# Retention scores and token transposes as 64 by 64 quarters of TensorE, with the decay put on q

## The chip, the core and the metric

One core of one Trainium2 chip runs the whole program once. The metric is the device time of one execution in microseconds (us); the median of three runs counts. On the core, TensorE (PE) multiplies matrices and writes to the eight banks of PSUM, VectorE (DVE) and ScalarE (ACT) read PSUM, GpSimd (POOL) works on SBUF alone, and SyncE (SP) issues most transfers. Each engine takes its instructions in program order and waits on semaphores for the others.

## What is computed

Three stages follow each other: retention (linear attention with a decay per head), a top-1 mixture of eight experts, and a dense layer with squared ReLU. The change lies in the first.

```python
# retention: B, H, S, D = 8, 8, 576, 64
scores = scale * np.matmul(q, k.transpose(0, 1, 3, 2))
gamma = 1.0 - 2.0 ** (-5.0 - np.arange(H))
Dmat = np.where(rel >= 0, gamma[:, None, None] ** rel, 0.0)      # rel = query - key position
x = matmul(scores * Dmat, v)                                     # -> 4608 tokens of 512 features
# experts: N, D, E, F = 4608, 512, 8, 1024
logits = x @ w_gate + modality_bias[modality_id]
out[token] = gate_w * (relu(x @ w1[e]) @ w2[e])                  # e = argmax(logits)
# dense: h = relu(x @ w_in); return h * h @ w_out
```

## The kernel before

The retention stage is `phase0`. The 4608 tokens are 36 tiles (`t`) of 128 tokens; 9 tiles hold 2 sequences of 576, so tile 4 of each 9 (`tt == 4`) holds the end of one sequence and the start of the next. The 512 features are four chunks `c` of 128, each with two heads `i` of 64. Four tiles make a group `g` for loading (`alloc`, `load`: k and q transposed, v and k natural, 1 MB each) and for routing (`route_a` to `route_c`). All products of this stage are of 32-bit floats, and each appears as two weight loads and two matmuls in the trace (so 8 products are "x16").

Per tile, TensorE does five things. `qk(t)` (L507) forms the scores of each head: 64 rows by 128 columns of the array, so two products side by side, 128 columns moving. DVE masks them into `at` (L510), two instructions of 512 elements. `om(t)` first adds the state product (L528), 64 by 64 quarters, four side by side, then scores times values (L534), 128 by 64. DVE multiplies the result by the decay `odec` into `xt` (L542, L545). `kv(t)` (L561) updates the state, which ACT copies to `sbs` (L564). `xm(t)` (L577) multiplies `xt` by `iwg`, an identity beside the gate's weights: a full 128 by 128 product with 136 columns moving for each chunk, which turns the tokens to rows and yields the logits. ACT copies the logits to `lp` (L579) and the tokens to `xs` (L580). POOL scales the values into `vh` (L500) and, in `prep`, builds `bias` and `trib` (L617 to L627).

The loop of L645 runs t from 0 to 36. In iteration t the order on every engine is: loads of a group ahead (where t % 4 is 1), `qk(t+1)`, `om(t)`, `kv(t)`, the steps that `stage` holds for this iteration (`route_c`, L252, four full-array products of 288 columns), `xm(t-1)`. The routing of a group, `route_a` (15 steps, mostly small DVE instructions, with an exponential and four `xs` scalings L199 to L207 on ACT) and `route_b` (10 steps; the first is a pair of products L215 and L216 into a bank of the ring of banks 6 and 7), is handed out in small parts: `adv(n)` runs n steps, three inside `qk` after each mask and three after `om`. After `xm(4g+3)` in iteration 4g+4 `route_a(g)` is queued, two iterations later `route_b(g)`, and in iteration 4g+8 `route_c(g)` runs.

At the end (t = 32 to 36) the routing of group 7 runs in one go, its table gives the first expert (`early`), and POOL gathers that expert's first tokens (`gather("E")`, four indirect transfers L453 after the copy of L450). `phase12` begins with their transposes (L768) and the expert's first products (L815). The later stages, 185 us to the end, are not touched by the change other than through the order of the rows of w1, which is permuted outside the kernel.

Of the kernel before, what the change touches and what calls it, by code (L numbers as in the profile page):

```python
# [32 lines left out]
LC = P + NE  # L33
# [11 lines left out]
def consts():  # L45
# [9 lines left out]
    od[1::2] = od[1::2, ::-1].copy()  # L55
# [36 lines left out]
def kernel(ctx, tc, qT, kT, kN, vN, modT, w_gate, mbias, w1, w2, w_in, w_out,  # L92
# [16 lines left out]
    banks = [bp.tile([P, TS], F32, name=f"bank{i}") for i in range(8)]  # L109
# [14 lines left out]
    psX = Banks(g=[6, 7])  # L124
    ring = [psX]
# [21 lines left out]
    def bc(ap, shape):  # L147
        return ap.to_broadcast(shape)
# [62 lines left out]
    def route_b(g, eng):  # L211
        t0 = G * g
        oh, pm = OH[g]
        ps = ring[0].tile([P, G, NE], F32, tag="g", name="psr")
# [42 lines left out]
    def tab_turn():  # L257
        tf = s1.tile([P, KEYS], F32, tag="tf", name="tf")
        ti = s1.tile([KEYS // 3, 3, P], I32, tag="ti", name="ti")
        dve.tensor_scalar(out=tf, in0=tps, scalar1=IDOFF, scalar2=None, op0=ALU.add)  # L260
        yield
        ps = ring[0].tile([P, 3, P], F32, tag="g", name="pst3")[:KEYS // 3]
        for j in range(3):
            pe.transpose(ps[:, j, :], tf[:, KEYS // 3 * j:KEYS // 3 * (j + 1)], ident)
        yield
        dve.tensor_copy(ti, ps)
        sp.dma_start(td.rearrange("(j k) b -> k j b", j=3), ti)
        yield

    def count(t, name):  # L270
        ps = ring[0].tile([P, NE], F32, tag="g", name=name)
        pe.matmul(ps, trib[:, 1, :], acc[:, t, :], start=True, stop=True, skip_group_check=True)
        return ps
# [183 lines left out]
    def phase0():  # L457
        with ExitStack() as c0:
# [13 lines left out]
            sps = psY.tile([P, KD, D], F32, tag="y3", name="sps")  # L472
# [21 lines left out]
            def qk(t, adv):  # L494
                b_, a, vn, kn = U[t // 4]
                x = t % 4
                cs = slice(x * P, x * P + P)
                at = wk.tile([P, H, P], F32, tag="at", name="at")
                vh = wk.tile([P, H, D], F32, tag="vh", name="vh")
                pool.tensor_tensor(out=vh, in0=vn[:, x, :].rearrange("p (h d) -> p h d", h=H),  # L500
                                   in1=bc(vdec[:, t % 9, :].unsqueeze(2), [P, H, D]), op=ALU.mult)
                mk = mask[:, 1 if t % 9 == 4 else 0, :]
                ps = [psY.tile([P, KD, P], F32, tag=f"y{i}", name=f"psa{i}") for i in range(2)]
                for c in range(KD):
                    for i in range(2):
                        r0 = 64 * i
                        pe.matmul(ps[i][:, c, :], b_[r0:r0 + 64, c, cs], a[r0:r0 + 64, c, cs],  # L507
                                  start=True, stop=True, skip_group_check=True)
                for i in range(2):
                    dve.tensor_tensor(out=at[:, KD * i:KD * i + KD, :], in0=ps[i],  # L510
                                      in1=bc(mk.unsqueeze(1), [P, KD, P]), op=ALU.mult)
                    adv(3)
                AT[t], VH[t] = at, vh
# [3 lines left out]
            def om(t):  # L517
                b_, a, vn, kn = U[t // 4]
                x = t % 4
                at, vh = AT[t], VH[t]  # L520
                pso = [banks[i][:, :2 * P].rearrange("p (c t) -> p c t", c=2) for i in (2, 5)]
                tt = t % 9
                ns = 0 if tt == 0 else (64 if tt == 4 else P)
                sb = sbs[scur[0]]
                for a2 in range(0, KD if ns else 0, 2):
                    for c, i in ((a2, 0), (a2 + 1, 1), (a2 + 1, 0), (a2, 1)):
                        o = 64 * (i ^ (c & 1))
                        pe.matmul(pso[c & 1][o:o + 64, c // 2, :ns], sb[64 * i:64 * i + 64, c, :],  # L528
                                  a[64 * i:64 * i + 64, c, x * P:x * P + ns], start=(a2 == 0), stop=False,
                                  skip_group_check=True)  # L530
                for c in range(KD):
                    for o in (0, 64):
                        i = (o // 64) ^ (c & 1)
                        pe.matmul(pso[c & 1][o:o + 64, c // 2, :], vh[:, 2 * c + i, :], at[:, KD * i + c, :],  # L534
                                  start=(c < 2 and not ns), stop=(c >= 2), skip_group_check=True)
                xt = wk.tile([P, KD, P], F32, tag="xt", name="xt")
                xv = xt.rearrange("p (c b) t -> p b c t", b=2)
                p0 = (t * P) % S
                n = min(P, S - p0)
                for b in range(2):  # L540
                    od = odec[:, b::2, :]
                    dve.tensor_tensor(out=xv[:, b, :, :n], in0=pso[b][:, :, :n], in1=od[:, :, p0:p0 + n],  # L542
                                      op=ALU.mult)
                    if n < P:
                        dve.tensor_tensor(out=xv[:, b, :, n:], in0=pso[b][:, :, n:], in1=od[:, :, 0:P - n],  # L545
                                          op=ALU.mult)
                XT[t] = xt

            def kv(t):
# [3 lines left out]
                b_, a, vn, kn = U[t // 4]  # L553
                x = t % 4
                vh = VH[t]
                r0 = 64 if tt == 4 else 0
                new = tt in (0, 4)
                for c in range(KD):
                    for i in range(2):
                        h = 2 * c + i  # L560
                        pe.matmul(sps[64 * i:64 * i + 64, c, :], kn[r0:, x, h * D:h * D + D], vh[r0:, h, :],  # L561
# [4 lines left out]
            def xm(t):  # L566
                g, j = t // G, t % G
                if j == 0:
                    XS[g] = wp.tile([P, G, DM], F32, tag="w", name="xs")
                    LP[g] = sm.tile([P, G, KD, NE], F32, tag="lp", name="lp")  # L570
                xt = XT.pop(t)
                xs = XS[g][:, j, :].rearrange("p (c d) -> p c d", c=KD)
                for a in range(2):
                    ps = psX.tile([P, 2, LC], F32, tag="g", name="psx")
                    for i in range(2):
                        c = 2 * a + i
                        pe.matmul(ps[:, i, :], xt[:, c, :], iwg[:, c, :], start=True, stop=True,  # L577
                                  skip_group_check=True)
                    act.activation(LP[g][:, j, 2 * a:2 * a + 2, :], ps[:, :, P:], AF.Copy)  # L579
                    act.activation(xs[:, 2 * a:2 * a + 2, :], ps[:, :, :P], AF.Copy)  # L580
# [3 lines left out]
            load(0, 0, 1, both, (0, 1))  # L584
            load(0, 1, 1, both, (0, 1))
            sp.dma_start(mask, mats_d[:, 0:2 * P].rearrange("p (a b) -> p a b", a=2))
            act.dma_start(vdec, vdec_d)
            load(0, 0, 1, both, (2, 3))
            sp.dma_start(odec[:, :, 0:P], odec_d[:, :, 0:P])
            act.dma_start(ident, mats_d[:, 2 * P:3 * P])  # L590
            for i in range(2):
                wgs = w_gate.rearrange("(c b p) e -> p c b e", b=2, p=64)
                for b in range(2):
                    act.dma_start(iwg[64 * i:64 * i + 64, b::2, P:], wgs[:, b::2, i ^ b])
            load(0, 1, 1, both, (2, 3))
            load(0, 2, 2, parts=(0, 1))
            sp.dma_start(odec[:, :, P:256], odec_d[:, :, P:256])
# [7 lines left out]
            noadv = lambda n: None  # L605
            qk(0, noadv)
            for c in range(KD):
                if c % 2 == 0:
                    pool.tensor_copy(iwg[:, c, :P], ident)
                else:  # L610
                    pool.tensor_copy(iwg[:, c, :64], ident[:, 64:])
                    pool.tensor_copy(iwg[:, c, 64:P], ident[:, :64])
# [32 lines left out]
            for t in range(NTILE + 1):  # L645
# [9 lines left out]
                if t == 2:  # L655
                    work.append(prep())
                if t + 1 < NTILE:
                    qk(t + 1, adv)
                if t < NTILE:
                    om(t)  # L660
# [18 lines left out]
                    kv(t)  # L679
                for it, fn in list(stage.items()):  # L680
                    if it == t:
                        fn()
                if t >= 1 and t - 1 != xl_:
                    xm(t - 1)
                    g, j = (t - 1) // G, (t - 1) % G
                    if j == G - 1 and g < NG - 2:
                        work.append(wrap(route_a(g)))
                        stage[t + 2] = lambda g=g: work.append(wrap(route_b(g, dve)))
                        stage[t + 4] = lambda g=g: (adv(99), route_c(g))

    def phase12():
        ring[0] = psG
# [681 lines left out]
def lay_out(i):  # L1374
    c = np.ascontiguousarray
    vdec, odec, mats, rows, _ = consts()
    tr = lambda a: c(a.transpose(1, 3, 0, 2)).reshape(DM, NT)
    nat = lambda a: c(a.transpose(0, 2, 1, 3)).reshape(NT, DM)
    return {
        "qT": tr(i['q']), "kT": tr(i['k']), "kN": nat(i['k']), "vN": nat(i['v']),  # L1380
        "modT": c(i['moe_modality_id'].astype(np.int64).reshape(NTILE, P).T),
        "w_gate": c(i['moe_w_gate']), "mbias": c(i['moe_modality_bias']),
        "w1": c(i['moe_w1']), "w2": c(i['moe_w2']),
# [18 lines left out]
```

## Time and profile before

| | us |
|---|---|
| median of 3 runs (1371.52 to 1373.61) | 1372.58 |
| the profiled execution | 1375.41 |
| its span, first to last instruction | 1373.6 |
| PE busy in the span | 1334.8 (97%) |
| DVE, ACT, POOL busy | 1022.4, 627.4, 131.0 |
| granted clock, mean | 0.995 |

A timeline row gives the start, the time that it is busy, the engine, the line, the operation, the tiles and how many instructions are merged. The busy time of a matmul row holds the modelled end of the last one; the time that a kind of work takes TensorE is the distance from its start to the start of the next row. Rows of one line are merged over an engine's neighbouring instructions. A row of the grouped view gives the count, the total, the mean of one in ns, and the idle time of the engine just before with what ended it.

### The profile page before, as it was taken

The page shows a single profiled execution, that of the slowest core. Times are in us where ns is not written, and L with a number is a line of the kernel's source. Part 1 is how long each engine was busy: PE and PEld are TensorE (multiplying, and loading weights), DVE is VectorE, ACT ScalarE, POOL GpSimd, SP SyncE. Part 2 cuts the span into 40 slices and gives each one's busy share as a digit, 9 for nine tenths or more (in the row PEclk, how much of TensorE's full clock was granted, in tenths as well). Part 3 has the DMA queues.
Part 4 walks back from the last instruction along what each step waited for, and adds up shares of the span by engine and source line. Part 5 has one row for each costly group of instructions (what it writes and reads, how often), then busy time and mean ns, then how long its engine had stood idle before and what let it go on. Part 6 is the DMA issues. An engine that isn't in the chain of part 4 may idle for free.

```text
span 1373.6 us, 26947 instructions
## 1 busy us (share of the span) xinstructions
PE 1334.8 (97%) x10643; PEld 1228.3 (89%) x10643; DVE 1022.4 (74%) x2077; ACT 627.4 (46%) x1283; POOL 131.0 (10%) x170
## 2 busy tenths in 40 slices
PE   6999999999999999999999999999999999999997
PEld 5888877888888888879999999999999999999997
DVE  2787857878787787554888888867887777776765
ACT  1444444454445445444655555543344344443333
POOL 3222114101110110000000000000000011111121
PEclk9999999999999999999999999999999999999999
DMA  9988256778786886669545554577799756564451
GB/s 332 386 303 295 91 195 231 272 278 283 246 288 236 302 277 216 240 232 342 226 187 207 211 212 185 207 269 270 288 337 339 279 229 209 200 213 170 169 183 48
DMA packets 139380, 332.55 MB, mean 242 GB/s; under 512 B 15568, under 2 KB 50160, under 8 KB 139248
## 3 DMA queue, kind: packets, MB, share of 16 engines
q1 hardware_dynamic: 131120, 310.21, 63.1%
q0 software_dynamic: 5920, 19.40, 4.0%
q8 instruction: 84, 1.38, 0.4%
q10 hardware_dynamic: 2208, 1.17, 0.3%
q14 instruction: 48, 0.39, 0.1%
HBM read 222.59 MB, written 108.17 MB: 241 GB/s over the span
## 4 chain that ended last, share of the span: by engine, by line
PE 47%; DMA 3%; DVE 2%; ACT 0%; issue 0%; POOL 0%; SPq 0%; POOLq 0%
PE bank L1176 16%; PE bank L1174 16%; PE bank L1175 16%; DMA w<-wc 3%; DVE z L1152 1%; DVE h L1277 0%; DVE z L1160 0%; ACT h L1276 0%; POOL out L1284 0%; SPq L1047 0%; DVE oe L1152 0%; ACT z L1149 0%; DVE x L1152 0%; DVE yr L1152 0%; POOLq L1398 0%
## 5 line engine op out<-in xcount | busy, mean ns | idle before, releaser
L1174 PE MATMUL bank<-x,w 128*128 128x256 f32 x1008 | 285.9, 284 | 1.2 <-ACT z L1149 1.1
L1175 PE MATMUL bank<-w,h 128*128 128x256 f32 x1008 | 282.8, 281 | 3.7 <-DMA w<-wc 3.7
L1175 PE MATMUL bank<-x,w 128*128 128x256 f32 x1008 | 285.8, 284 | 0.5 <-DVE x L1152 0.5
L1174 PE MATMUL bank<-w,h 128*128 128x256 f32 x1008 | 282.7, 280 | 2.9 <-DVE oe L1152 1.6
L1176 PE MATMUL bank<-x,w 128*128 128x256 f32 x1008 | 285.0, 283 | 0.0
L1176 PE MATMUL bank<-w,h 128*128 128x256 f32 x1008 | 282.2, 280 | 0.7 <-DVE h L1277 0.7
L1149 ACT ACTIVATE z<-bank 128x256 f32<-128x256 f32 x288 | 108.7, 380 | 255.5 <-PE bank L1176 253.5
L1174 PEld LDWEIGHTS bank<-x,w 128*128 128x128 f32 x1008 | 192.6, 191 | 2.7 <-ACT z L1149 2.7
L1276 ACT ACTIVATE h<-z 128x512 fp32r<-128x512 f32 (+2 forms) x270 | 158.2, 598 | 80.0 <-DVE z L1152 63.7
L1175 PEld LDWEIGHTS bank<-x,w 128*128 128x128 f32 x1008 | 192.9, 191 | 1.1 <-DVE x L1152 0.7
L1174 PEld LDWEIGHTS bank<-w,h 128*128 128x128 f32 x1008 | 190.0, 189 | 4.0 <-DVE oe L1152 2.2
L1175 PEld LDWEIGHTS bank<-w,h 128*128 128x128 f32 x1008 | 189.6, 188 | 4.4 <-DMA w<-wc 4.3
L1176 PEld LDWEIGHTS bank<-x,w 128*128 128x128 f32 x1008 | 193.1, 192 | 0.0
L1176 PEld LDWEIGHTS bank<-w,h 128*128 128x128 f32 x1008 | 189.7, 188 | 0.9 <-DVE h L1277 0.9
L1277 DVE TENSOR_TENSOR h<-z,h 128x512 fp32r<-128x512 f32 (+2 forms) x270 | 168.7, 648 | 7.8 <-ACT h L1276 7.8
L1152 DVE TENSOR_TENSOR z<-z,bank 128x256 f32<-128x256 f32 x216 | 89.2, 416 | 68.8 <-PE bank L1176 50.0
L815 PE MATMUL bank<-hh,wy 128*128 128x512 f32 (+1 forms) x320 | 125.3, 392 | 0.0
L815 PE MATMUL bank<-xh,wx 128*128 128x512 f32 (+1 forms) x320 | 122.9, 384 | 1.7 <-DVEq L934 1.7
L816 PE MATMUL bank<-xl,wx 128*128 128x512 f32 (+1 forms) x320 | 122.7, 383 | 1.1 <-DVE xl L771 1.1
L817 PE MATMUL bank<-xh,wx 128*128 128x512 f32 (+1 forms) x320 | 123.5, 386 | 0.0
L817 PE MATMUL bank<-hh,wy 128*128 128x512 f32 (+1 forms) x320 | 123.3, 385 | 0.0
L816 PE MATMUL bank<-hl,wy 128*128 128x512 f32 (+1 forms) x320 | 122.6, 383 | 0.0
(172 smaller groups left out, 2135.9 us busy)
## 6 DMA issues: line engine op xcount, KB each, us to landing
x<-xc SPq DMA_DIRECT2D x112, 512.0 KB
wr<-w SPq DMA_DIRECT2D x80, 512.0 KB
xc<-x SPq DMA_DIRECT2D x63, 512.0 KB
w<-wc SPq DMA_DIRECT2D x32, 896.0 KB
wc<-cwh SPq DMA_DIRECT2D x16, 896.0 KB
wc<-cwl SPq DMA_DIRECT2D x16, 896.0 KB
pd<-oe SPq DMA_DIRECT2D x24, 512.0 KB
xd<-xs SPq DMA_DIRECT2D x9, 1024.0 KB
```

The source lines that it names most:

```text
L815: pe.matmul(ps, lh, rh, start=first, stop=False)
L816: pe.matmul(ps, lh, rl, start=False, stop=False)
L817: pe.matmul(ps, ll, rh, start=False, stop=last)
L1149: plan.add(a_(c), lambda e: e.activation(o, i, f), r, w)
L1152: plan.add(engs or d_(c), lambda e: e.tensor_tensor(out=o, in0=a, in1=b, op=op), r, w)
L1174: e.matmul(ps[n], lh, rh, start=first and n == 0, stop=False, skip_group_check=True)
L1175: e.matmul(ps[n], lh, rl, start=False, stop=False, skip_group_check=True)
L1176: e.matmul(ps[n], ll, rh, start=False, stop=True, skip_group_check=True)
L1276: plan.add(a_(c), lambda e: e.activation(h[:, 0, a:b], z[:, a + 1:b + 1], AF.Copy), rs, ks[0])
L1277: plan.add(d_(c), lambda e: e.tensor_tensor(out=h[:, 1, a:b], in0=z[:, a + 1:b + 1], in1=h[:, 0, a:b].bitcast(F32), op=ALU.subtract), rs + ...
```

## The change

`qk` computes the scores in quarters: for each chunk and head, and each half `h` of the 128 keys, a 64 by 64 product with 128 columns moving; 16 products in place of 8. `xm` does the same for the tokens: for each chunk, half of the tokens and head, a 64 by 64 product with 72 columns moving (64 of an identity, 8 of the gate); 16 in place of 4. `iwg` comes ready from the host, and the gate's partial logits double (`lp` has 2 * KD parts). The order in an iteration becomes `ahead(t+2)`, `qk(t+1)`, `sq_(t)` (the state product), `adv(6)`, `stage`, `xm(t-1)`, `om(t)` (scores times values), `kv(t)`, `adv(3)`. The decay is no longer multiplied into `xt`: `ahead` multiplies it into q, in place, on DVE for the first four tiles and on POOL after that, and also makes `vh`, two iterations before the tile's own. `xt` becomes one ACT copy of 512 elements out of two banks, and the copies of `xm` become one of 64 and one of 512 elements. The banks are laid out anew: scores 0 and 1, result 2 and 3, state 5, tokens and logits 6 and 7, the small routing products in the rest of bank 6. The first transfers are reordered, with the first piece of `odec` ahead of the second tile.

```diff
-LC = P + NE
+LC = D + NE
...
-    psX = Banks(g=[6, 7])
-    ring = [psX]
+    def route_bank(shape, name):
+        if side[0]:
+            n = int(np.prod(shape[1:]))
+            ps = banks[6][:, KD * LC:KD * LC + n]
+            return ps.rearrange("p (a b) -> p a b", b=NE) if len(shape) == 3 else ps
+        return psG.tile(shape, F32, tag="g", name=name)
...
+            psa = bank[:, 0:2, :].rearrange("p i (c t) -> p i c t", c=KD)
+            pso = bank[:, 2:4, :2 * P].rearrange("p b (c t) -> p b c t", c=2)
+            sps = banks[5][:, :KD * D].rearrange("p (c d) -> p c d", c=KD)
+            psx = bank[:, 6:8, :KD * LC].rearrange("p b (c e) -> p b c e", c=KD)
...
+            def ahead(t):
+                if t < NTILE:
+                    a = U[t // 4][1][:, :, t % 4 * P:t % 4 * P + P]
+                    e = dve if t < 4 else pool
+                    p0 = (t * P) % S
+                    n = min(P, S - p0)
+                    e.tensor_tensor(out=a[:, :, :n], in0=a[:, :, :n], in1=odec[:, :, p0:p0 + n], op=ALU.mult)
+                    if n < P:
+                        e.tensor_tensor(out=a[:, :, n:], in0=a[:, :, n:], in1=odec[:, :, 0:P - n], op=ALU.mult)
+                    vh = VH[t] = wk.tile([P, H, D], F32, tag="vh", name="vh")
+                    pool.tensor_tensor(out=vh, in0=U[t // 4][2][:, t % 4, :].rearrange("p (h d) -> p h d", h=H),
+                                       in1=bc(vdec[:, t % 9, :].unsqueeze(2), [P, H, D]), op=ALU.mult)
...
+                for c in range(KD):
+                    for h in range(2):
+                        ks = slice(t % 4 * P + 64 * h, t % 4 * P + 64 * h + 64)
+                        for i in range(2):
+                            pe.matmul(psa[64 * h:64 * h + 64, i, c, :], b_[D * i:D * i + D, c, ks],
+                                      a[D * i:D * i + D, c, cs], start=True, stop=True, skip_group_check=True)
                 mk = mask[:, 1 if t % 9 == 4 else 0, :]
...
-                    dve.tensor_tensor(out=xv[:, b, :, :n], in0=pso[b][:, :, :n], in1=od[:, :, p0:p0 + n],
-                                      op=ALU.mult)
...
+                xt = XT[t] = wk.tile([P, 2, 2, P], F32, tag="xt", name="xt")
+                act.activation(xt, pso, AF.Copy)
...
+                for c in range(KD):
+                    for h in range(2):
+                        for r in range(2):
+                            pe.matmul(psx[64 * h:64 * h + 64, r, c, :],
+                                      xt[D * r:D * r + D, c & 1, c // 2, 64 * h:64 * h + 64],
+                                      iwg[D * r:D * r + D, c, :], start=True, stop=True, skip_group_check=True)
+                act.activation(LP[g][:, j].rearrange("p (r c) e -> p r c e", r=2), psx[:, :, :, D:], AF.Copy)
+                act.activation(XS[g][:, j, :].rearrange("p (r c d) -> p r c d", r=2, c=KD), psx[:, :, :, :D], AF.Copy)
...
+                ahead(t + 2)
                 if t + 1 < NTILE:
-                    qk(t + 1, adv)
+                    qk(t + 1)
                 if t < NTILE:
-                    om(t)
+                    ns = sq_(t)
+                    adv(6)
+                for it, fn in list(stage.items()):
+                    if it == t:
+                        fn()
+                if t >= 1 and t - 1 != xl_:
+                    xm(t - 1)
...
+                if t < NTILE:
+                    om(t, ns)
+                    kv(t)
```

## Rows read from the trace of the kernel before

**Rows 1.** Busy time by stretch: bounds, length, then each engine's, clock, DMA.

```profile
35.00:153.00 118.00, 117.28 (x1886) 103.67 (x1884) 89.88 (x302) 49.20 (x164) 28.22 (x27) 1.00 0.81 293
```

**Rows 2.** Timeline of TensorE, iterations 20 and 21: start, busy time, instructions.

```profile
107.83 0.79 PE L252 MATMUL bank<-okb 128*128 128x288 f32 x4
108.46 1.09 PE L577 MATMUL bank<-iwg,xt 128*128 128x136 f32 x8
109.48 1.16 PE L507 MATMUL bank<-q,k 64*128 64x128 f32 x16
110.57 0.67 PE L528 MATMUL bank<-q,sbs 64*64 64x128 f32 x16
111.17 1.09 PE L534 MATMUL bank<-at,vh 128*64 128x128 f32 x16
112.09 0.64 PE L561 MATMUL bank<-vh,kn 128*64 128x64 f32 x16
112.66 1.19 PE L577 MATMUL bank<-iwg,xt 128*128 128x136 f32 x8
113.78 0.49 PE L507 MATMUL bank<-q,k 64*128 64x128 f32 x3
```

**Rows 3.** Timeline of TensorE, iteration 31 (state product with 64 columns).

```profile
152.91 1.16 PE L507 MATMUL bank<-q,k 64*128 64x128 f32 x16
...
154.15 0.46 PE L528 MATMUL bank<-q,sbs 64*64 64x64 f32 x16
154.54 1.09 PE L534 MATMUL bank<-at,vh 128*64 128x128 f32 x16
...
158.58 1.16 PE L507 MATMUL bank<-q,k 64*128 64x128 f32 x16
```

**Rows 4.** Groups of instructions by line and shape, 35 to 153 us.

```profile
L510 DVE TENSOR_TENSOR at<-bank,mask 128x512 f32<-128x512 f32 x54 | 36.8, 684 | 26.6 <-PE bank L507 26.6
...
L500 POOL TENSOR_TENSOR vh<-v,vdec 128x512 f32<-128x512 f32 x27 | 28.3, 1047 | 90.0 <-PE bank L561 59.5 <-issue 21.5 <-PE bank L534 5.6
...
L580 ACT ACTIVATE xs<-bank 128x256 f32<-128x256 f32 x53 | 19.8, 380 | 0.0
L542 DVE TENSOR_TENSOR xt<-bank,odec 128x256 f32<-128x256 f32 x48 | 17.9, 413 | 0.0
...
L202 ACT ACTIVATE xs<-xs,gg 128x512 f32<-128x512 f32 x7 | 4.9, 707 | 0.0
```

**Rows 5.** Waits, 35 to 153 us: who for whom, total us, times, longest.

```profile
PE bank L215 <- ACT xs L580: 0.7, 1, 0.7
```

**Rows 6.** Timeline, a POOL instruction beside a small one of DVE.

```profile
94.81 1.04 POOL L500 TENSOR_TENSOR vh<-v,vdec 128x512 f32<-128x512 f32 x1 [3.32 <-issue]
95.01 0.89 DVE L180 TENSOR_TENSOR sh<-lg,mx 128x32 f32<-128x32 f32 x1
```

**Rows 7.** All instructions of L180: shortest, median and longest, ns.

```profile
L180 DVE TENSOR_TENSOR sh<-lg,mx x9: 180/183/890, 42.2 to 193.5; 128x32 f32<-128x32 f32 x9
```

**Rows 8.** Timeline, the start of the stage.

```profile
23.36 0.40 POOL L617 CAST trib<-trio 128x256 bf16<-128x256 f32 x1 [4.09 <-DMA trio<-mats]
...
25.11 0.79 POOL L627 TENSOR_TENSOR bias<-bias,bias 128x288 f32<-128x288 f32 x1
...
28.87 1.47 PE L507 MATMUL bank<-q,k 64*128 64x128 f32 x16 [3.41 <-DMA q<-qT]
...
31.58 3.23 POOL L500 TENSOR_TENSOR vh<-v,vdec 128x512 f32<-128x512 f32 x3 [5.68 <-DMA v<-vN]
...
34.73 1.16 PE L507 MATMUL bank<-q,k 64*128 64x128 f32 x16
```

**Rows 9.** Timeline, the end of the stage and the first expert.

```profile
171.43 0.19 POOL L450 COPY ix<-tab 128x4 int32 x1 [13.98 <-DVE eslot L298]
...
177.39 1.05 POOL L500 TENSOR_TENSOR vh<-v,vdec 128x512 f32<-128x512 f32 x1
178.49 0.85 PEld L534 LDWEIGHTS bank<-at,vh 128*64 128x64 f32 x16 [3.04 <-POOL vh L500]
...
183.11 1.95 PE L768 MATMUL bank<-ident,xg 128*128 128x128 f32 x16
184.81 0.48 PE L815 MATMUL bank<-xh,wx 128*128 128x512 f32 x1
```

More of the change, by code (lines that the diff above doesn't have):

```diff
@@ L107 @@
     s1 = cm.enter_context(tc.tile_pool(name="s1", bufs=1))
-    banks = [bp.tile([P, TS], F32, name=f"bank{i}") for i in range(8)]
+    bank = bp.tile([P, 8, TS], F32, name="bank")
+    banks = [bank[:, i, :] for i in range(8)]
     class Banks:
@@ L261, in tab_turn @@
         yield
-        ps = ring[0].tile([P, 3, P], F32, tag="g", name="pst3")[:KEYS // 3]
+        ps = psG.tile([P, 3, P], F32, tag="g", name="pst3")[:KEYS // 3]
         for j in range(3):
@@ L509, in qk, with sq_ @@
                 for i in range(2):
[L510 to L513, printed above, removed]
+                    dve.tensor_tensor(out=at[:, i], in0=psa[:, i], in1=bc(mk.unsqueeze(1), [P, KD, P]), op=ALU.mult)
             scur = [0]
[L517 to L521, printed above, removed]
+            def sq_(t):
+                a = U[t // 4][1]
@@ L569, in xm @@
                     XS[g] = wp.tile([P, G, DM], F32, tag="w", name="xs")
-                    LP[g] = sm.tile([P, G, KD, NE], F32, tag="lp", name="lp")
+                    LP[g] = sm.tile([P, G, 2 * KD, NE], F32, tag="lp", name="lp")
                 xt = XT.pop(t)
[L572 to L580, printed above, removed]
+                for c in range(KD):
[6 more added lines that the diff above has]
+                act.activation(XS[g][:, j, :].rearrange("p (r c d) -> p r c d", r=2, c=KD), psx[:, :, :, :D], AF.Copy)
             alloc(0)
@@ L584, in phase0 @@
             load(0, 0, 1, both, (0, 1))
+            sp.dma_start(odec[:, :, 0:P], odec_d[:, :, 0:P])
+            act.dma_start(vdec, vdec_d)
+            act.dma_start(mask, mats_d[:, 0:2 * P].rearrange("p (a b) -> p a b", a=2))
+            load(0, 0, 1, both, (2, 3))
             load(0, 1, 1, both, (0, 1))
[L586 to L594, printed above, removed]
+            sp.dma_start(odec[:, :, P:256], odec_d[:, :, P:256])
+            act.dma_start(iwg, iwg_d.rearrange("p (c e) -> p c e", c=KD))
             load(0, 1, 1, both, (2, 3))
             load(0, 2, 2, parts=(0, 1))
-            sp.dma_start(odec[:, :, P:256], odec_d[:, :, P:256])
+            act.dma_start(ident, mats_d[:, 2 * P:3 * P])
             load(0, 2, 2, parts=(2, 3))
@@ L604, in phase0 @@
             dve.memset(acc[:, 0, :], 0.0)
[L605 to L612, printed above, removed]
+            ahead(0)
+            qk(0)
+            ahead(1)
             alloc(1)
@@ L656, in phase0 @@
                     work.append(prep())
+                ahead(t + 2)
                 if t + 1 < NTILE:
-                    qk(t + 1, adv)
+                    qk(t + 1)
                 if t < NTILE:
-                    om(t)
+                    ns = sq_(t)
[5 more added lines that the diff above has]
+                    xm(t - 1)
+                    g, j = (t - 1) // G, (t - 1) % G
+                    if j == G - 1 and g < NG - 2:
+                        work.append(wrap(route_a(g)))
+                        stage[t + 2] = lambda g=g: work.append(wrap(route_b(g, dve)))
+                        stage[t + 4] = lambda g=g: (adv(99), route_c(g))
+                if t < NTILE:
+                    om(t, ns)
+                    kv(t)
                     if t == xl_ + 2:
@@ L678, in phase0 @@
                             pass
[L679 to L689, printed above, removed]
     def phase12():
-        ring[0] = psG
+        side[0] = False
         with ExitStack() as c1:
```

64 lines of the change are left out of this document (24 added, 40 removed).

## The prediction, before the changed kernel was run

> **What bounds the kernel now.** I read the busy time by stretch first. From 35 to 153 us, where the retention loop runs undisturbed, TensorE is busy 117.28 of 118.00 us at full clock, DVE 89.88, ACT 49.20, POOL 28.22 [rows 1]. So time falls where TensorE's work falls, until DVE's 76% becomes the bound. Then I read TensorE's timeline: the distance from one row to the next is what a kind of work takes. Iteration 21 is a plain one: scores 1.09 us, state product 0.60, scores times values 0.92, state update 0.57, tokens 1.12; together 4.30 [rows 2]. Twenty-seven iterations (4 to 30) lie between 34.73 and 152.91, so 118.2 us [rows 3, 8].
>
> **What one quarter costs.** The state product already runs in quarters, 16 instructions with 128 columns in 0.60 us; in iteration 31 the same 16 with 64 columns take 0.39 [rows 2, 3]. Four run side by side, so these are four rounds: 64 columns less save 0.21 / 4 = 0.053 us a round. A round of 128 columns is thus 0.107 us, and 0.60 - 4 x 0.107 = 0.17 us is what entering and leaving this tiling costs. (Full-size tokens: 8 x 136 columns at this rate are 0.91 of 1.12 us, which leaves 0.21 for the switch; scores in halves leave 0.23.)
>
> **TensorE per iteration, after.** Scores: 32 instructions, 8 rounds of 0.107 = 0.86. State product: 4 rounds, 0.43. Tokens: 32 instructions, 8 rounds of 72 columns, 0.060 each by the same slope, 0.48. One entry and exit for the three, 0.17. Then 0.92 + 0.57 unchanged. Sum 3.43 us; I take 3.45, as short rounds hardly run at the bare slope. The scores alone gain nothing (0.86 for 1.09 - 0.23); the gain is two switches and the tokens' columns: 0.85 us an iteration, 23.0 in 27. Three of these (t = 9, 18, 27) have no state product and so one switch less to save: -0.5.
>
> **Routing products between.** `route_c` now stands between two quarter stages. Before, it cost 0.63 and shortened the tokens from 1.12 to 1.02 [rows 2], 0.53 net. After, it leaves and re-enters the quarters: 0.63 + 0.17 = 0.80. Six of them: -1.6. Its operands are ready: with adv(3) in the iteration that queues the work and nine steps in each later one, `route_a` and `route_b` end in iteration 4g+7, one ahead of it.
>
> **DVE** loses two instructions of 413 ns and keeps two of 684 [rows 4], so it falls by 0.8 us of 3.3 an iteration, to some 2.6 of 3.45: no bound.
>
> **ACT** gains one copy of 512 out of PSUM. Two of 256 take 2 x 380 ns and the scaling of 512 takes 707 [rows 4]; I take 0.6, bounds 0.5 to 0.8. The copy is hidden behind the state update, the next scores and state product (0.57 + 0.86 + 0.43) before the next `xm` reads it. But ACT is in order, and once per group four scalings stand ahead. Counted from the start of iteration 4g+5: the masks end at 2.4, the exponential that waits behind them at 3.0; tokens' copies 0.6, `xt` 0.5, state 0.3, four scalings 2.5 (they follow each other faster than their 707), tokens' copies 0.6: 7.5. The pair L215 and L216 needs these last copies out of bank 6, and TensorE reaches it at 2 x 3.45 = 6.9. Before, that wait was 0.7 us in all [rows 5]. New wait: 0.55 x 7 = -3.9, bounds 0 and 8. Behind it on TensorE stand the scores of the next tile.
>
> **POOL** gains the decay, 512 elements from two SBUF operands, of which no row shows one; `vh` of that size takes 1047 ns with one operand broadcast [rows 4], and 288 elements of two plain operands 0.79 us [rows 8]. In proportion that is 1.4; as both hold a fixed part, I take 1.2. Two such instructions are 2.25 of 3.45 us, bounds 2.1 to 2.5: not the bound. `vh` waits for the state update that frees its buffer [rows 4]; both run from the start of an iteration, a tile or more ahead of use.
>
> [...] A DVE instruction of 128 x 32 that takes 183 ns took 890 when POOL was at `vh`, and ended 0.05 us after it [rows 6, 7]. [...] From the rows: DVE's routing steps come behind the masks, 2.4 us into an iteration, when POOL's 2.25 are over. So I charge nothing; if that cover fails, it is the rival on the slow side.
>
> **The start** is bound by transfers: the scores of tile 4 wait for q until 28.87 [rows 8]. After, POOL's `ahead(4)` first decays it, then waits for v (31.58), takes 1.04, and `prep`, which had run early, stands behind: 25.11 + 0.79 - 23.36 = 2.5 us [rows 8]. Then the decay of tile 5, 1.2: 36.3, and 0.4 for the larger `iwg` ahead in the queues. Iteration 4 starts at 36.7 instead of 34.73: -2.0, bounds 0 and -4. The decays on DVE for tiles 0 to 3 hide in the same wait.
>
> **The end.** Iteration 31 with the tokens of tile 31 takes 5.67 us [rows 3]; after, 3.45 + 0.17 + 0.48 + 0.2 of wait = 4.3: +1.3. From there to the first expert product is 26.2 us (158.58 to 184.81) [rows 3, 9], a chain of routing, table, gather. Off this chain go DVE's decay instructions, 0.7 + 0.5, so the gather starts 12.85 - 1.2 = 11.65 after tile 31. Its four transfers hold POOL until 177.39, 5.96 us, and `vh(35)` stood behind them, for which TensorE waited 3.04 [rows 9]; after, `vh(35)` is made two iterations ahead. What remains is the landing, some 2, and the transposes, 1.7 [rows 9]: 11.65 + 5.96 + 3.7 = 21.3, so +4.9; some part of a window at half clock may follow the idle time, so +4.2, bounds 1.2 (the chain alone) and 5.
>
> **Sum:** 23.0 - 0.5 - 1.6 - 3.9 - 2.0 + 1.3 + 4.2 = 20.5 us. Against the profiled execution (1375.41; 1.8 of it lie outside the span of 1373.6) that gives 1354.9. It is 2.8 above the median of 1372.58, so the forecast is **1352**. The bounds of the unknown terms (ACT wait 0 to 8, start 0 to 4, end 1.2 to 5) and 1 us for small waits give 1345 to 1360 for this case.
>
> **Rivals.** (1) *Copies late on every tile.* ACT now frees the result banks, the token banks and the state. If each iteration waited 0.55 instead of one in four, 27 x 0.55 = 15 instead of 3.9, so 11 less gain: 1363. For it: three releases in one queue. Against it: ACT's 49.2 of 118 us [rows 1] grows to about 2.4 of 3.45 an iteration, with slack in three of four.
>
> (2) *Short quarters don't run four wide.* If a round of 72 columns cost what one of 128 does, tokens are 0.86 instead of 0.48: 0.38 x 28 = 10.6 less gain: 1363. The 64-column rows speak against it: 0.39 - 0.17 is 0.055 a round [rows 3]. [...]
>
> (3) [...] A group has four pairs of masks, 8 x 0.684 = 5.5 us, and routing, (89.88 / 27 - 1.37 - 0.8) x 4 = some 4.7 [rows 1, 4]. If POOL's 9 us a group fell on DVE's small steps in full, DVE would take 19.2 us a group, 4.8 an iteration against 4.38 now: 27 x 0.42 = 11.3 slower, less 2.2 at start and end: 1382. Such waits eat into the gain from 3.6 us a group (four iterations of 3.45) and turn it into a loss from 7.3. Against it: the order of the two in time, above.
>
> (4) *No change.* If instruction supply or transfers set a pace near today's 4.3, start and end alone remain, -2.0 + 4.2: 1370.
>
> **How the numbers follow.** Forecast 0.67, (1) 0.12, (2) 0.09, (3) 0.06, (4) 0.06. 0.2% (2.7 us) is what a measurement here tells from no change. Faster by more: the forecast, (1) and (2), 0.88; within: (4), 0.06; slower: 0.06. Rivals (3) and (4) may be left out and a little of the forecast's tails: low 1344, high 1364.
>
> **What would show it.** Right: a plain iteration of 3.4 to 3.5 us; scores, state and tokens with one 0.17 us switch; tokens near 0.5; the pair L215 and L216 waiting for ACT about once per group; iteration 4 near 36.7; no wait of TensorE for `vh(35)`. Wrong: `sq_` or `xm` waiting for ACT in plain iterations (1), tokens near 0.8 (2), DVE's 128 x 32 steps at 0.5 us and more and scores waiting for masks (3), TensorE idle without a releaser (4).

## The result and the profile after

The changed kernel takes 1385.8 us (median) against 1372.05 beside it: ratio 1.0104 [1.0077, 1.0131], slower. A second time, on another chip, it was 1388.2 against 1371.1: 1.0139 [1.0110, 1.0168] (1383 to 1388 us had been expected there). The profiled execution has a span of 1384.3 us against 1373.6.

First the loop, by stretch (columns as in [rows 1]): iterations 4 to 31 of the changed kernel, then a piece of it.

```profile
36.64:171.08 134.44, 109.15 (x2971) 97.72 (x2967) 81.21 (x243) 59.31 (x141) 64.19 (x60) 0.95 0.71 254
61.40:64.80 3.40, 3.40 (x64) 3.28 (x64) 0.33 (x1) 0.98 (x2) 2.15 (x2) 0.50 1.05 394
```

The 27 iterations took 118.2 us before [rows 3, 8] and take 134.4 now. TensorE, busy nearly all the time in [rows 1], is idle for 25.3 of 134.4 us. Its granted clock is 0.95 in the mean: after some of the idle times, not all, it is 0.50, four times for 3.4 us. The second row is such a stretch, behind the 3.36 us of idle time that end at 60.94; behind the 2.39 us that end at 53.04 the products run at full speed.

Yet a plain iteration is as short as forecast. Timeline of TensorE, one of them (to be set beside [rows 2]):

```profile
75.06 1.10 PE L524 MATMUL bank<-q,k 64*64 64x128 f32 x32
75.98 0.62 PE L540 MATMUL bank<-q,sbs 64*64 64x128 f32 x16
76.42 0.68 PE L579 MATMUL bank<-iwg,xt 64*64 64x72 f32 x32
77.03 1.09 PE L550 MATMUL bank<-at,vh 128*64 128x128 f32 x16
77.95 0.63 PE L565 MATMUL bank<-vh,kn 128*64 128x64 f32 x16
78.52 1.10 PE L524 MATMUL bank<-q,k 64*64 64x128 f32 x32
```

From row to row: scores 0.92, state 0.44, tokens 0.61, values 0.92, update 0.57; together 3.46 us. (Each fp32 product is two records, each with its weight load.)

The time went into holes, stretches in which TensorE does nothing. The same timeline, some 25 us earlier:

```profile
46.62 0.60 PE L579 MATMUL bank<-iwg,xt 64*64 64x72 f32 x21 [0.82 <-issue]
47.14 1.09 PE L550 MATMUL bank<-at,vh 128*64 128x128 f32 x16
48.06 0.64 PE L565 MATMUL bank<-vh,kn 128*64 128x64 f32 x16
48.63 1.10 PE L524 MATMUL bank<-q,k 64*64 64x128 f32 x32
49.55 0.62 PE L540 MATMUL bank<-q,sbs 64*64 64x128 f32 x16
49.99 0.66 PE L579 MATMUL bank<-iwg,xt 64*64 64x72 f32 x27
53.04 0.35 PE L579 MATMUL bank<-iwg,xt 64*64 64x72 f32 x5 [2.39 <-issue]
...
56.93 0.66 PE L550 MATMUL bank<-at,vh 128*64 128x128 f32 x8
60.94 0.71 PE L550 MATMUL bank<-at,vh 128*64 128x128 f32 x8 [3.36 <-issue]
...
62.44 1.98 PE L524 MATMUL bank<-q,k 64*64 64x128 f32 x31
```

"issue" means that the engine waited for nothing the profile shows. Add up the counts between two holes: 21 + 16 + 16 + 32 + 16 + 27 = 128 products, with their weight loads 256 instructions. The holes fall in the middle of a kind of work, where no operand is due, and every hole over 1 us in the loop that has no releaser stands a whole number of 256 instructions from the others (to within the one record in some hundred that a trace misses). At 53.04 and 60.94 there are 6.4 and 7.9 us from hole to hole; an iteration of 224 instructions would use up 256 in 3.95. The last row runs at half clock: 1.98 us where 1.10 is usual.

The DMA view has a queue of kind "instruction". Its rows (packets, MB, share) for [rows 1]'s stretch before, and for iterations 4 to 31 after:

```profile
q8 instruction: 15, 0.25, 0.8%
```

```profile
q8 instruction: 24, 0.39, 1.2%
```

A packet is 16 KB, which over the 256 instructions counted between holes comes to 64 bytes each; I call it a block. Before, one was due every 7.9 us; after, without holes, it would be every 3.95. In the records of that queue after the change, the block that is missing at 57.6 us (the one before it had been entered at 53.04) begins its transfer at 58.49, takes 0.90, and TensorE goes on at 60.94: 5.4 us until the transfer starts, 0.9 for it, 1.6 until work. Behind the holes that end at 40.29 and 46.62, too, the next transfer starts only after the entry, at 44.14 and 50.50: in all three a block is fetched once the one before it runs.

Second, the waits of TensorE in the loop (who for whom, total us, times, longest), products and then a weight load:

```profile
PE bank L579 <- issue: 8.3, 5, 2.6
PE bank L550 <- issue: 5.0, 2, 3.4
PE bank L258 <- DVE okb L250: 4.2, 4, 1.1
PE bank L524 <- issue: 3.0, 1, 3.0
PE bank L540 <- issue: 2.3, 1, 2.3
PE bank L221 <- ACT xs L583: 1.7, 4, 0.6
...
PEld bank L258 <- DVE okb L250: 7.6, 13, 1.3
```

For the products, "issue" comes to 18.6 us. Next in size is `route_c` (L258, the "bin matmuls" of the experiments), which waits for the last eight steps of `route_b` (L248 and L250, here the "one-hot steps"). Timelines of DVE, POOL and TensorE around one:

```profile
78.08 0.29 DVE L248 TENSOR_SCALAR okb<-rows,bb 128x128 fp32r<-128x128 f32 x1
...
78.62 0.28 DVE L248 TENSOR_SCALAR okb<-rows,bb 128x128 fp32r<-128x128 f32 x1
78.82 1.15 DVE L250 TENSOR_SCALAR okb<-rows,ky 128x288 fp32r<-128x288 f32 x1
79.89 1.29 DVE L248 TENSOR_SCALAR okb<-rows,bb 128x128 fp32r<-128x128 f32 x1
81.10 0.42 DVE L250 TENSOR_SCALAR okb<-rows,ky 128x288 fp32r<-128x288 f32 x1
...
78.74 1.06 POOL L513 TENSOR_TENSOR vh<-v,vdec 128x512 f32<-128x512 f32 x1 [1.76 <-PE bank L565]
79.77 1.33 POOL L509 TENSOR_TENSOR q<-q,odec 128x512 f32<-128x512 f32 x1
...
81.58 0.93 PE L258 MATMUL bank<-okb 128*128 128x288 f32 x2 [1.06 <-DVE okb L250]
```

The step that takes 0.42 us takes 1.15 when POOL is at `vh`, and the one of 0.28 takes 1.29 when POOL is at the decay; each ends 0.1 to 0.2 us after POOL's. `route_c` then takes 2.45 us (79.99 to 82.44) instead of 0.63 [rows 2].

Third, the end (timeline of TensorE and POOL; to be set beside [rows 3, 9]):

```profile
171.08 1.10 PE L524 MATMUL bank<-q,k 64*64 64x128 f32 x32
...
176.80 0.36 PE L579 MATMUL bank<-iwg,xt 64*64 64x72 f32 x8 [1.56 <-issue]
176.97 1.50 PE L524 MATMUL bank<-q,k 64*64 64x128 f32 x32
...
189.89 0.18 POOL L456 COPY ix<-tab 128x4 int32 x1 [6.46 <-DVE at L528]
...
197.12 0.33 PE L767 MATMUL bank<-ident,xg 128*128 128x128 f32 x1 [1.98 <-DMA xg<-xd,ix]
...
202.97 0.77 PE L814 MATMUL bank<-xh,wx 128*128 128x512 f32 x1
```

Iteration 31 to the first expert product: 31.9 us, as before (152.91 to 184.81). So the first expert product is 18.2 us later, of which 1.9 arose before iteration 4 and 16.3 in the loop. What follows it took 1181.4 us instead of 1188.8. I don't count these 7 us as the change's: two kernels below, e9_halves_end and e10_halves_start, have the same code there and differ by 6 (1182.0 and 1188.1), on two chips. So the loss is 18.2 us up to the first expert product, 10.7 by the two spans and 13.8 by the medians; what makes the last part shorter is not shown.

### The profile page after: what moved, and what is told of

It is laid out like the page before. It is cut to its first block, busy times and chain, and to the rows that moved or that the text cites. A ratio compares the mean times of both kernels' runs of the same rounds, so it can differ in the third digit from the quotient of the medians.

```text
span 1384.3 us, 29755 instructions
## 1 busy us (share of the span) xinstructions
PE 1319.2 (95%) x12083; PEld 1218.1 (88%) x12083; DVE 1013.9 (73%) x2001; ACT 641.1 (46%) x1247; POOL 167.3 (12%) x200
## 3 DMA queue, kind: packets, MB, share of 16 engines
q8 instruction: 95, 1.56, 0.5%
## 4 chain that ended last, share of the span: by engine, by line
PE 50%; DVE 2%; DMA 1%; POOL 0%; issue 0%; POOLq 0%; DVEq 0%
PE bank L1174 16%; PE bank L1173 16%; PE bank L1175 16%; DMA w<-wc 1%; DVE z L1151 1%; DVE h L1276 1%; PE bank L814 0%; PE bank L816 0%; PE bank L815 0%; DVE z L1159 0%; POOL out L1283 0%; DVE oe L1151 0%; DVE x L1151 0%; DVE yr L1151 0%; POOLq L1402 0%
```

## The experiments

All figures of a row but the last two are from one profiled execution; the times come from several chips, so the ratios decide. "issue" is the idle time of TensorE's products under that name in iterations 4 to 31; "L258" the sum of the six sections of bin matmuls there, each from its first row to the next kind of work (before: 0.62 to 0.75 each); "end" runs from iteration 31 to the first expert product.

| kernel | TensorE instr. per iteration | iteration 4 at | 4 to 31 | issue | L258 | end | us | ratio to before |
|---|---|---|---|---|---|---|---|---|
| before | 144 | 34.7 | 118.2 | 0 | 3.9 | 31.9 | 1372.1 | |
| after | 224 | 36.6 | 134.4 | 18.6 | 12.2 | 31.9 | 1385.8 | 1.0104 |
| after_again | 224 | 36.1 | 133.3 | 17.5 | 12.2 | 31.7 | 1388.2 | 1.0139 |
| e1_light | 224 | 36.5 | 116.8 | 2.3 | 15.2 | 31.8 | 1371.9 (one run) | |
| e2_dve_decay | 224 | 36.7 | 131.7 | 17.4 | 9.7 | 32.0 | 1393.2 | 1.0146 |
| e3_halves | 192 | 34.8 | 124.0 | 8.2 | 9.4 | 33.8 | 1380.5 | 1.0057 |
| e4_paced | 224 | 37.3 | 123.1 | 10.2 | 10.9 | 32.9 | 1382.2 | 1.0065 |
| e5_late_c | 224 | 36.3 | 132.2 | 24.5 | 4.3 | 34.4 | 1388.9 | 1.0139 |
| e6_paced_late | 224 | 37.2 | 124.4 | 20.5 | 4.3 | 33.6 | 1379.1 | 1.0071 |
| e7_two_halves | 160 | 37.1 | 113.6 | 0 | 4.3 | 37.4 | 1374.0 | 1.0025 |
| e8_light_late | 224 | 35.9 | 111.6 | 3.1 | 4.3 | 34.1 | 1366.7 (one run) | |
| e9_halves_end | 160 | 38.0 | 113.8 | 0 | 4.3 | 34.8 | 1370.1 | 0.9999 |
| e10_halves_start | 160 | 34.5 | 113.8 | 0 | 4.3 | 35.0 | 1372.7 | 0.9975 |

**Theory:** blocks of 256 instructions come late because their transfer stands behind the loads; next to it, POOL's work stretches DVE's one-hot steps. **Rivals:** a supply rate of its own, whatever else moves; operand waits that the trace doesn't name; and, for L258, one-hot steps that are late only because they are queued late.

**Loads away (e1_light).** `VP` is the buffer of v of the first group, which stands in for v and natural k of the later ones.

```diff
+            VP = U[0][2] = cp.tile([P, 4, TS], F32, name="vp")
...
-                    alloc(u)
-                    load(u, 4 * u, 4)
+                    if u < 3:
+                        alloc(u)
+                        load(u, 4 * u, 4)
+                    else:
+                        U[u] = U[u - 3][:2] + [VP, VP]
```

> Changed kernel without the four 1 MB transfers of each of groups 3 to 8 of the retention (their loads are left out and data of earlier groups is used again, so the output is not the reference's). First theory, TensorE's instruction blocks arrive late because they share the DMA engines with the loads: the idle stretches of TensorE with no semaphore behind them (about 24 us, each at a multiple of 256 of its instructions) go, iterations 4 to 31 take about 112 to 116 us instead of 134.4, the whole about 1365. The waits of the bin matmuls at L258 on DVE stay (about 11 us). Rival one, the blocks come at a rate of their own whatever else moves: the stretches stay and so do 134 us. Rival two, the stretches are operand waits that the trace doesn't name: those of loads go, but not at the multiples of 256.

The waits of TensorE's products in the loop, the loop by stretch, and its instruction queue:

```profile
PE bank L258 <- DVE okb L250: 6.4, 6, 1.1
PE bank L221 <- ACT xs L583: 4.2, 7, 1.4
PE bank L540 <- issue: 2.3, 1, 2.3
```

```profile
36.48:153.24 116.76, 102.72 (x2970) 92.39 (x2967) 84.56 (x243) 58.02 (x141) 63.20 (x59) 0.99 0.21 74
```

```profile
q8 instruction: 24, 0.39, 1.3%
```

Same instructions, same 24 blocks, DMA share 0.21 instead of 0.71, and one hole of nine is left, at 38 us, while loads still run. "Issue" falls from 18.6 to 2.3 us and the loop to 116.8 (112 to 116 expected). So the first theory holds against its rivals. What the loads delay is the start of a fetch and not the transfer (records of that queue): in the changed kernel the next block's transfer starts 3.9 to 5.4 us after the entries at 40.29, 46.62 and 53.04, with loads all the while (DMA share 1.04 to 1.07 from entry to start), but 1.1 us after those at 90.24 and 111.33 (0.11 and 0.14), and it takes 0.9 to 1.3 us in both cases. But L258 now costs 15.2 us, all six sections 2.45 or more: in the changed kernel a late block had given some of the one-hot steps time to end (its first section took 0.71). So without late blocks the loop is only 1.4 us shorter than before the change, and the one time, 1371.9, is above the 1365 expected.

**Decay on DVE (e2_dve_decay).**

```diff
-                    e = dve if t < 4 else pool
+                    e = dve
```

> Changed kernel with the decay of q on VectorE for every tile, as before; all else as changed. First theory, GpSimd's decay and v product stretch VectorE's one-hot steps (0.28 and 0.42 us alone, 1.15 to 1.38 beside GpSimd) and the bin matmuls wait for them, six times about 1.8 us: with GpSimd's work halved the sections at L258 take 1.0 to 1.6 us instead of 2.45, iterations 4 to 31 about 128 instead of 134.4 us, the whole 1378 to 1382; the idle stretches at the multiples of 256 instructions stay. Rival, the one-hot steps are late because they are queued late, and the decay on VectorE (about 1.2 us an iteration) makes them later still: L258 takes 2.5 us or more and the whole is 1386 to 1395.

L258 falls by 2.5 us and the loop by 2.7, but the time isn't shorter: 1.0146 [1.0129, 1.0163], not told apart from the change's own two ratios. Each theory was right in part: the sections take 1.6 us in the mean, as the first had it, and the time is the rival's. Moving the decay back to DVE doesn't win the loss back. The mean of the steps at L248 (36 to 160 us) fell from 467 to 310 ns, which ties the stretching to POOL's work, yet most of what L258 takes stays.

**Scores in halves (e3_halves).**

```diff
-                    for h in range(2):
-                        ks = slice(t % 4 * P + 64 * h, t % 4 * P + 64 * h + 64)
-                        for i in range(2):
-                            pe.matmul(psa[64 * h:64 * h + 64, i, c, :], b_[D * i:D * i + D, c, ks],
-                                      a[D * i:D * i + D, c, cs], start=True, stop=True, skip_group_check=True)
+                    for i in range(2):
+                        pe.matmul(psa[:, i, c, :], b_[D * i:D * i + D, c, cs],
+                                  a[D * i:D * i + D, c, cs], start=True, stop=True, skip_group_check=True)
```

> Changed kernel with the scores in 64 by 128 halves as before (8 products instead of 16 in quarters), tokens and state in quarters: 192 TensorE instructions an iteration instead of 224, one tiling switch more, some 0.3 to 0.5 us more work an iteration. First theory, instruction supply: a block of 256 lasts about 4.9 us instead of 3.95 against the 6.4 that a block needs beside the loads, so the idle stretches shrink from about 24 to about 10 us while the work grows by 8 to 13 us: iterations 4 to 31 take 129 to 135 us, the whole 1380 to 1386. Rival, the stretches do not hang on the count of instructions: they stay, and the whole is 1393 to 1399.

Plain iterations 3.68 us instead of 3.46, "issue" 8.2 instead of 18.6, loop 124.0, below the 129 expected at best: more work, less time. With e1_light, where the same 224 instructions leave one hole, this says that the count costs while loads run.

**Loads paced (e4_paced).**

```diff
-                    load(u, 4 * u, 4)
+                if 2 + (t - 1) // 4 < 9 and t >= 1:
+                    u = 2 + (t - 1) // 4
+                    load(u, 4 * u, 4, (act, act, act, act), ((t - 1) % 4,))
```

> Changed kernel with the four 1 MB transfers of a group issued one an iteration from ScalarE's queue instead of four at once from SyncE's: same bytes, same instructions of TensorE. If a block's fetch waits behind the transfers that are queued at that moment, a shallower queue lets it start sooner: the idle stretches fall from 24 to under 10 us and the whole to 1368 to 1375. If it is slowed only by the share of the engines over the whole stage (the mean share is 0.8), the stretches stay near 24 us and the whole at 1383 to 1389; loads that come too late would show as waits of the scores on DMA.

"Issue" nearly halves, to 10.2; the loop falls by 11.3. The time, 1382.2, is far from the 1368 to 1375 of the first case. So how the loads are issued matters, with the same bytes at a DMA share of 0.80, but blocks are still late. The edit changes two things at once, how many loads are queued and whose queue they stand in; which of the two helped is not shown.

**Bin matmuls an iteration later (e5_late_c), and with paced loads (e6_paced_late).**

```diff
-                        stage[t + 4] = lambda g=g: (adv(99), route_c(g))
+                        stage[t + 4] = lambda: adv(99)
+                        stage[t + 5] = lambda g=g: route_c(g)
```

> Changed kernel with the bin matmuls of a routing group (L258) one iteration later; the one-hot steps of VectorE stay where they were, so they have an iteration to end in. First theory, the waits at L258 are late operands alone: the sections take about 0.65 us instead of 0.7 to 2.8 (sum 13.4, so 9 us less), iterations 4 to 31 take 125 to 127 instead of 134.4, the whole 1376 to 1379. Rival, a block of instructions that is late anyway was hidden behind these waits, so the idle stretches at the multiples of 256 grow by what the waits lose: iterations 4 to 31 at 130 to 134, the whole 1381 to 1386.

> Changed kernel with the bin matmuls one iteration later and a group's loads issued one an iteration from ScalarE's queue. If the two causes add up (pacing took iterations 4 to 31 from 134.4 to 123.1 with 11.5 us in the sections at L258, of which 7 were waits), they take about 116 us and the whole 1374 to 1377. If one hides behind the other, 120 to 123 us and 1379 to 1382.

The rival came nearer both times, though e5_late_c is slower than either range and the loop of e6_paced_late 1.4 us above its own. The waits at L258 are gone, 7.9 us of them, and "issue" grows from 18.6 to 24.5: the loop is 2.2 us shorter and the ratio that of after_again on the same chip. With paced loads "issue" goes from 10.2 to 20.5 and the loop from 123.1 to 124.4. So most of a wait was free here while blocks were late, as it would be if the next block comes nearer meanwhile.

**Both away (e8_light_late)**: e1_light and e5_late_c together.

> Changed kernel without the loads of groups 3 to 8 (data of earlier groups is used again, so the output is not the reference's) and with the bin matmuls one iteration later: both suspected costs away at once. If the instruction blocks and the one-hot steps are all that the change lost in the loop, the waits at L258 (sections of 2.45 us to 0.72, 11 us in sum) go now in full, since no late block hides behind them: iterations 4 to 31 at 105 to 107 us against 116.8 with the loads alone away and 132.2 with the bin matmuls alone late; the whole about 1361. If a third cost sits in the loop, iterations 4 to 31 stay over 110.

111.6, so a third cost sits in the loop. Timelines of DVE and TensorE:

```profile
86.03 1.15 DVE L250 TENSOR_SCALAR okb<-rows,ky 128x288 fp32r<-128x288 f32 x1
87.10 1.30 DVE L248 TENSOR_SCALAR okb<-rows,bb 128x128 fp32r<-128x128 f32 x1
88.33 0.42 DVE L250 TENSOR_SCALAR okb<-rows,ky 128x288 fp32r<-128x288 f32 x1
...
89.20 1.28 DVE L528 TENSOR_TENSOR at<-bank,mask 128x512 f32<-128x512 f32 x2
...
90.03 1.49 PE L524 MATMUL bank<-q,k 64*64 64x128 f32 x29 [0.83 <-DVE at L528]
```

The masks stand behind the eight one-hot steps, two of which are stretched by 0.7 and 1.0 us, and the scores of the next tile wait for the masks: 4.6 us in the loop, in five groups. This is the sign of rival (3) of the prediction, in small.

**Fewer instructions, same idea (e7_two_halves)**: scores as in e3_halves, bin matmuls as in e5_late_c, and the token turns in halves right behind the scores (`xm` moved ahead of `sq_`), so that two tilings an iteration are kept.

```diff
-                    for h in range(2):
-                        for r in range(2):
-                            pe.matmul(psx[64 * h:64 * h + 64, r, c, :],
-                                      xt[D * r:D * r + D, c & 1, c // 2, 64 * h:64 * h + 64],
-                                      iwg[D * r:D * r + D, c, :], start=True, stop=True, skip_group_check=True)
+                    for r in range(2):
+                        pe.matmul(psx[:, r, c, :], xt[D * r:D * r + D, c & 1, c // 2, :],
+                                  iwg[D * r:D * r + D, c, :], start=True, stop=True, skip_group_check=True)
```

> Changed kernel with scores and token turns in 64 by 128 halves one behind the other, then state product, values and state in quarters (two tilings an iteration as in the change, 144 TensorE instructions instead of 224, as before the change), bin matmuls one iteration later, loads as in the change. If the count of instructions is what the change paid for: hardly any idle stretch at the multiples of 256, plain iterations 3.5 to 3.8 us, iterations 4 to 31 about 105 to 112 us against 118.2 before the change, the whole 1360 to 1368. Rival, the quarters were what made the work short and the halves give it back: plain iterations 4.1 to 4.3 us and the whole 1370 to 1376.

The expectation miscounted: it is 160 instructions, not 144. Timeline of a plain iteration:

```profile
87.15 1.16 PE L522 MATMUL bank<-q,k 64*128 64x128 f32 x16
88.14 1.01 PE L576 MATMUL bank<-iwg,xt 64*128 64x72 f32 x16
89.08 0.67 PE L538 MATMUL bank<-q,sbs 64*64 64x128 f32 x16
89.68 1.09 PE L548 MATMUL bank<-at,vh 128*64 128x128 f32 x16
90.61 0.63 PE L563 MATMUL bank<-vh,kn 128*64 128x64 f32 x16
91.17 1.04 PE L522 MATMUL bank<-q,k 64*128 64x128 f32 x12
```

4.02 us, between the two expectations: token turns in halves take 0.94 where quarters take 0.61, the state product 0.60 for 0.44. But no hole is left; this is the only wait of its products in the loop:

```profile
PE bank L576 <- ACT xt L551: 0.7, 2, 0.4
```

The loop takes 113.6 us, 4.6 less than before the change and 20.8 less than after it. Start and end give it back: 2.3 and 5.5 us later than before, so the time is the rival's.

**Its end (e9_halves_end) and its start (e10_halves_start).** The first diff is against e7_two_halves, the second against e9_halves_end.

```diff
-                    e = dve if t < 4 else pool
+                    e = dve if t < 4 or t > 32 else pool
...
-                    adv(6)
+                    adv(6 if t < 29 else 9)
...
-                        stage[t + 4] = lambda: adv(99)
-                        stage[t + 5] = lambda g=g: route_c(g)
+                        if g < NG - 3:
+                            stage[t + 4] = lambda: adv(99)
+                            stage[t + 5] = lambda g=g: route_c(g)
+                        else:
+                            stage[t + 4] = lambda g=g: (adv(99), route_c(g))
```

> The kernel with scores and token turns in halves and two tilings, with its end tuned: decay of the last three tiles on VectorE, routing steps of the last groups taken nine instead of six at a time, the last group but one's bin matmuls not delayed. There the loop (113.6 us against 118.2 before the change) is kept and the end from iteration 31 to the first expert product (37.4 against 31.9, with TensorE at half clock after a wait for the routing steps that GpSimd stretched) should fall to 32 to 34: the whole 2 to 6 us under the unaltered end, so 0.0 to 0.4% under the kernel before. If the routing chain of the last group sets the end whatever is queued ahead of it, nothing is won and the ratio stays at 1.002 to 1.003.

```diff
+            sp.dma_start(odec[:, :, 256:384], odec_d[:, :, 256:384])
             load(0, 2, 2, parts=(2, 3))
-            sp.dma_start(odec[:, :, 256:S], odec_d[:, :, 256:S])
+            sp.dma_start(odec[:, :, 384:S], odec_d[:, :, 384:S])
```

> The kernel with halves, two tilings and the tuned end, and with the decay factors of tile 2 (the third quarter megabyte of odec) asked for ahead of v and k of tiles 2 and 3 instead of behind them. There VectorE's decay of tile 2 waited 8.3 us for that transfer and held the mask step of tile 1 behind it, so TensorE stood 4.75 us and iteration 4 began at 38.0 us, 3.3 later than before the change. If that wait sets the start, iteration 4 begins at 34 to 36 us and the whole is 2 to 3.5 us less than without it: ratio to before about 0.998. If the transfers of v and of the next group set it anyway, iteration 4 stays at 37 to 38 and the ratio at 1.000.

The end falls from 37.4 to 34.8 (32 to 34 expected), and the time is 0.9999 [0.9982, 1.0016] of before. The wait at the start could be avoided. Timeline of DVE in the changed kernel:

```profile
20.23 0.69 DVE L509 TENSOR_TENSOR q<-q,odec 128x512 f32<-128x512 f32 x1 [6.70 <-DMA odec<-odec]
20.84 1.28 DVE L528 TENSOR_TENSOR at<-bank,mask 128x512 f32<-128x512 f32 x2
```

The decay of tile 2 waits 6.7 us for its factors, which were asked for behind v and k of tiles 2 and 3, and the masks of tile 1 stand behind it on DVE. With that transfer earlier, iteration 4 starts at 34.5 instead of the 38.0 of e9_halves_end, and the kernel takes 0.9975 [0.9962, 0.9988] of before, as expected. It is the one version with all its loads that is faster than both the kernel before and the changed one.

## Why the prediction was wrong

**The step that failed** is the sum itself, where 0.85 us of TensorE's work an iteration became 27 x 0.85 = 23.0 us of time. It left out that 144 instructions become 224 and that these must be brought. With all terms of the sum the forecast loop was 118.2 - 23.0 + 0.5 + 1.6 + 3.9 = 101.2 us, and it took 134.4, so 33.2 more. Late blocks cost 18.6 of them before products (e1_light takes 16.3 away). The half clock behind some of the holes adds to it: 5% of 134.4 us is 6.7 at most. The bin matmuls cost 7.4 more than charged, the wait for ACT 2.2 less; together these come to 30.5 at most. The mechanism stood in rival (4) at 0.06, as a pace near 4.3; measured it was 4.98 (134.4 / 27), so not "no change" but a loss. What [rows 1] and the DMA view showed was the demand (15 blocks in 118 us, DMA share 0.81). The price of a block, about 6.4 us among loads, was hidden behind the 7.9 us that a block lasted, and I set none.

**"Its operands are ready"** was wrong too. The steps are handed to DVE in iteration 4g+7, as counted, but DVE runs them behind that iteration's masks: the first one-hot step starts at 78.08, 0.4 us before the iteration of its bin matmuls (78.52), and two of the eight are stretched by 1.7 us together. The six sections take 12.2 us instead of the 4.8 charged. Taking the waits away won 2.2 us of the loop here (e5_late_c), and 5.2 without late blocks (116.8 to 111.6).

**"So I charge nothing"** for POOL beside DVE: wrong. I looked at the 128 x 32 steps with two operands [rows 6, 7] and forgot L248 and L250, which have one. The trace of the kernel before had the sign: its step at L242, the later L248, takes 0.27 us as a rule and 1.11 at the longest. L248 takes 0.28 us alone and 1.29 beside POOL in the changed kernel; by what means POOL holds DVE up is not shown.

**The end**, +1.3 and +4.2, did not come: iteration 31 took 5.89 us instead of 4.3, with a hole of 1.56 us in it, and the gather starts 12.9 us after tile 31 as before (12.85), not 11.65. `vh(35)` no longer waits, as forecast, but the rows of the gather land 2 us later than TensorE wants them, and the 16 transposes take 5.9 instead of 1.7: three more waits for rows, 1.9 us together, and a granted clock of 0.50 (198.0 to 202.9) lie among them. What sets the landing of the rows I did not test. The 4.2 allows for half clock after idle time, which the trace before shows: 0.50 from 179.8 to 183.1 us, behind the wait for `vh(35)` [rows 9].

**Right:** the plain iteration (3.43 to 3.45 forecast, 3.46 measured), with it the rounds of four and the one switch; rival (2) is out: 32 token products take 0.61 us here, 19 ns each. The wait for ACT at L221: -3.9 forecast, 4.2 in e1_light, 1.7 where blocks hide it. Iteration 4 at 36.7 forecast, 36.64 measured, is luck: the factors of tile 2 were late (6.7 us) and a block too (1.26 us at 33.85), while TensorE waited neither for `prep` nor for the decay of tile 5.

**Open:** e8_light_late, with loads and bin waits away, has a loop of 111.6 against the 101.2, of which 4.6 are scores that wait for masks and 3.1 are holes. As its wait for ACT is 2.1 and not the 3.9 charged, some 4.5 us have no cause here. And the range was added up wrongly: 1352 with 4.1 for ACT, 2 for the start, 3 for the end and 1 for small waits is 1362, not the 1360 given for this case; against 1385.8 that changes nothing.

## What to carry to other kernels

When a change multiplies an engine's instructions, count them against the time they will take, and look at the instruction queue in the DMA view. That view gives the demand; what a block costs among loads shows only where one comes late. Here 256 instructions in 3.95 us were too fast among loads, 256 in 6.4 (e7_two_halves, 160 in 4.02) were not. Before removing a wait, look whether a late block hides behind it; here taking away 7.9 us of waits won 2.2. And an engine in order passes its wait on: one transfer asked for too late held masks, scores and the start.

## What the runs showed of the hardware

Blocks of 256 TensorE instructions came late while loads were queued: between holes among loads a block took 6.3 to 7.9 us from entry to entry, though its transfer took 0.9 to 1.1; with a DMA share of 0.21 (e1_light) instead of 0.71 one hole was left of nine. Scores of 128 columns cost nearly the same in quarters (0.92 us) as in halves (0.99 in e7_two_halves, 1.09 before, each with its change of tiling), but token products of 72 columns didn't: 0.61 in quarters, 0.94 in halves. Two of DVE's `tensor_scalar` steps (L250 and L248), with one fp32 operand in SBUF, ended 0.1 to 0.2 us after the POOL instruction that ran beside them, at 1.15 and 1.29 us instead of 0.42 and 0.28.
